# Attention and two expert layers on one core: new homes for S, P V and layer 1 in PSUM, joint transposes, a new order

## The chip, the cores and the metric

The kernel runs on one core of a Trainium2 chip. The metric is device time in microseconds of one execution. A core has TensorE (PE, with its weight load as PEld), VectorE (DVE), ScalarE (ACT), GpSimd (POOL) and SyncE (SP, which here only issues transfers); DVE, ACT and TensorE reach PSUM, which has eight banks of 512 float32 columns in each of 128 partitions.

## The reference, cut to what matters

```python
q_rot, k_rot = rotate(q), rotate(k)            # batch 4, heads 8, seq 576, head_dim 64
scores = matmul(q_rot, k_rot^T) / sqrt(64); scores -= max(scores)
attn = exp(scores); attn /= sum(attn) + 1e-9
x = matmul(attn, v)                            # as 2304 tokens x 512
h = x @ w_in;  g = h * clip(h + 3, 0, 6) / 6;  y = g @ w_out          # 512 -> 2048 -> 512
h = y @ w_in2; P = a0 + a1 h + a2 h^2 + a3 h^3; Q = 1 + |b0||h| + |b1| h^2
out = (P / (Q + 1e-6)) @ w_out2                                       # 512 -> 2048 -> 512
```

All inputs are float32. The kernel keeps the accuracy by splitting values into a high and a low half (16-bit in attention and layer 1, fp32r in layer 2) and multiplying high by high, high by low and low by high.

## The kernel before

**Attention.** The 8 heads of a batch are 4 pairs. `prep_qk` loads a pair's k and q (`nat`), sums their squares for a scale, rotates them on DVE (buffer `ropea`), writes the high and low halves of each into `qk16` and sends each through a DMA transpose (L818); `k2` is k with its halves swapped. `prep_v` splits v. `unit` is one block of 128 queries of both heads of a pair (a fifth unit of each pair takes the 64 last queries of both): S = q k into PSUM (L856), the row maximum on DVE (L862), one small operation on it (L864, on POOL), the exponential on ACT (L869, tile `e`), the high half `p16h` (L539, L541 or L543 by engine), the low half `p16l` on DVE (L881), a DMA transpose of each half (L878) and P V (L898, L901), whose result and row sums ACT or DVE copy to `xu`. There are 5 units for each of 16 pairs, 80 in all. `x_out` divides by the sums, splits x and transposes both halves (L937).

**Layer 1** (`layer1`) follows in two parts for each batch, of 256 and 320 columns: 16 blocks of 12 matmuls (L968), each taken out of PSUM by ACT (L972) and DVE (L974) and split into `gh` and `gl`; then 4 output groups of 48 matmuls (L992). Its weights are loaded as raw 32-bit words and decoded exactly by ACT and DVE (L636 to L639), then split (L646). **Layer 2** runs at the end, 5 blocks of columns by 16 steps, and reuses the memory of both.

**PSUM.** S has one tile of 2560 columns, five banks; unit i uses columns 0 to 1151 or 1280 to 2431 by turns:

```python
sbank = tl("psa", [128, 2560], F32, "s")
obank = tl("psa", [128, 512], F32, "ob")
c0 = 1280 * (i % 2)
```

One more bank, `ob`, holds P V at three places by turns and the results of small sums over partitions (`small`, `total`); layer 1 has two banks `h`.

**The order.** Every operation is given to a planner (`Plan`) with the engines that may run it, a cost for each and a due time in ticks of 4000 ns. `Plan.order` plays the program forward: each free engine takes the ready operation with the earliest due time, and a second engine of the list may take it at a penalty `pen`. The order that comes out is the order of the instructions in each engine's queue; what an instruction waits for on the chip is found from the data. The table `PR` holds the engines (`'GA'` is POOL, then ACT; Q is SP's queue), buffer numbers and shifts of the due times by operation (`o_...`, and `z_...` for the first batch). `EN(key)` takes the entry with a 0 at its end for the first two batches.

Of the kernel before, what the change touches and what calls it, by code (L numbers as in the profile page):

```python
# [22 lines left out]
S = 576  # L23
# [14 lines left out]
PR = {'c01': -1.023,  # L38
# [3 lines left out]
 'e_ev': 'AD',  # L42
 'e_ev0': 'AD',
 'e_gh': 'GD',
# [3 lines left out]
 'e_hi': 'ADG',  # L48
 'e_hi0': 'ADG',
 'e_mx': 'G',  # L50
 'e_mx0': 'G',
 'e_ob': 'A',
 'e_qk': 'GA',
 'e_qk0': 'GA',
# [6 lines left out]
 'e_v': 'DG',  # L61
 'e_v0': 'GAD',
 'e_vl': 'D',
 'e_vl0': 'D',
 'e_w': 'G',
 'e_wl': 'D',
 'e_wl0': 'D',
 'e_xh': 'A',
# [5 lines left out]
 'e_y': 'A',  # L74
 'e_y0': 'A',
# [5 lines left out]
 'l0q': 0.5,  # L81
 'l1o': 2.462,
 'l1p': -2.749,
 'lead': 14.779,
 'lead0': 7.701,
# [4 lines left out]
 'o_': -43.42,  # L90
 'o_ab': -2.87,
 'o_ac0': -118.75,
 'o_ac1': 0.34,
 'o_ac2': -86.97,
 'o_ac3': 94.5,
 'o_acc': 17.25,
 'o_bb': -12.47,
 'o_d': -49.02,
 'o_e': -40.44,
 'o_f32': -13.78,  # L100
 'o_g2l': -17.75,
 'o_gh': 39.63,
 'o_gl': 7.33,
 'o_h': 3.68,
 'o_h2': 12,
 'o_half': 66.6,
 'o_hh': 3.05,
 'o_hr': 11.75,
 'o_hx': 2.17,
 'o_ident': 138.79,  # L110
 'o_k2': 20.81,
 'o_lgh': 53.65,
 'o_lgl': -159.43,
 'o_lq': -53.65,
 'o_lr': -2.25,
 'o_ls': -34.29,
 'o_lt': 4.25,
 'o_mx': 12.06,
 'o_na': -45.2,
 'o_nat': 6.15,  # L120
 'o_ob': -0.02,
 'o_ones': 72.16,
 'o_p1': -5.5,
 'o_p16': 0.25,
 'o_p16h': 32.49,
 'o_p16l': 0.33,
 'o_pt': 6.74,
 'o_pth': -4.52,
 'o_ptl': -9.92,
 'o_pw': 35.47,  # L130
 'o_pwi': -44.5,
 'o_qal': -73.87,
 'o_qam': -26.95,
 'o_qb': -48.22,
 'o_qk16': 4.58,
 'o_qpi': -3.4,
 'o_qps': 10.25,
 'o_qpv': -48.65,
 'o_r': -29.58,
 'o_r0': 18,  # L140
 'o_raw': -4.11,
 'o_ropea': 20.61,
 'o_ropeb': 4.5,
 'o_s': -0.66,
 'o_so': -46.98,
 'o_t': -203.65,
 'o_t0': 28.3,
 'o_t1': 0.14,
 'o_tab': -87.11,
 'o_u': -23,  # L150
 'o_v9': 25.68,
 'o_vam': 118.58,
 'o_vm4': 36.12,
 'o_vnat': 9,
 'o_vnat0': 12.82,
 'o_vnat1': -27.04,
 'o_vpi': -56.08,
 'o_vps': -35.07,
 'o_vpv': -77.42,
 'o_vqi': 6.84,  # L160
 'o_vqs': -58.99,
# [24 lines left out]
 'o_y1d': -133.22,
# [28 lines left out]
 'w20': 109.798,  # L215
 'w21': 121.496,
# [3 lines left out]
 'wi0': -8.964,  # L220
 'wi1': 4.619,
 'wo0': -2.418,
 'wo1': 6.01,
 'y0': 2,
 'z_': 2.02,
 'z_ab': -15.43,
 'z_ac0': -6.16,
 'z_ac1': -16.43,
 'z_ac2': -25.19,
 'z_ac3': -7.09,  # L230
 'z_acc': 0.0,
 'z_bb': 20.23,
 'z_d': 16.19,
 'z_e': 1.8,
 'z_f32': 8.07,
 'z_g2h': 0.0,
 'z_gh': -14.04,
 'z_gl': -0.51,
 'z_h': 0.0,
 'z_h2': 0.0,  # L240
 'z_half': -10.82,
 'z_hh': -8.5,
 'z_hr': 0.0,
 'z_hx': 3.93,
 'z_ident': -8.76,
 'z_k2': 26.21,
 'z_lgh': -1.25,
 'z_lgl': 17.55,
 'z_lq': 6.06,
 'z_lr': -1.93,  # L250
 'z_ls': -16.45,
 'z_lt': -3.17,
 'z_mx': -0.03,
 'z_na': -20.82,
 'z_nat': -0.01,
 'z_ob': 0.06,
 'z_ones': -25.61,
 'z_p1': 0.0,
 'z_p16': 0.0,
 'z_p16h': -11.01,  # L260
 'z_p16l': 0.0,
 'z_pt': 0.0,
 'z_pth': 0.89,
 'z_ptl': -8.13,
 'z_pw': 2.56,
 'z_pwi': -3.9,
 'z_qal': 0.48,
 'z_qam': 3.82,
 'z_qb': -8.89,
 'z_qk16': -5.39,  # L270
 'z_qpi': 6.81,
 'z_qps': -13.66,
 'z_qpv': -1.31,
 'z_r': 5.16,
 'z_r0': 0.0,
 'z_raw': 3.72,
 'z_ropea': 0.0,
 'z_s': 0.0,
 'z_so': 2.72,
 'z_t': -13.02,  # L280
 'z_t0': 2.23,
 'z_t1': -0.22,
 'z_tab': 1.34,
 'z_u': 0.0,
 'z_v9': -0.53,
 'z_vam': 22.59,
 'z_vm4': -1.37,
 'z_vnat': 0.0,
 'z_vnat0': -0.34,
 'z_vnat1': 11.21,  # L290
 'z_vpi': 3.94,
 'z_vps': 2.18,
 'z_vpv': -0.76,
 'z_vqi': 0.09,
 'z_vqs': -3.6,
 'z_vqv': -0.13,
 'z_vv': 0.0,
 'z_w0_': -1.91,
 'z_w1_': -1.69,
 'z_w2_': -11.93,  # L300
 'z_w2d': -53.68,
 'z_w2s': 0.31,
 'z_wam': 0.46,
 'z_wao': -23.4,
 'z_woi': -19.0,
 'z_wos': -20.61,
 'z_wov': -28.27,
 'z_wpi': 19.44,
 'z_wps': 3.61,
 'z_x20': -25.98,  # L310
 'z_x21': -5.61,
 'z_xf': 0.57,
 'z_xh': -0.37,
 'z_xl': -1.14,
 'z_xn': 0.0,
 'z_xt': -3.31,
 'z_xu': 0.87,
 'z_y0': 0.0,
 'z_y1': 0.65,
 'z_y1d': 19.64}  # L320
# [13 lines left out]
class Til:  # L334


    def __init__(self, plan, pool, shape, dtype, tag, bufs):
        self.plan, self.pool, self.shape, self.dtype, self.tag, self.bufs = plan, pool, shape, dtype, tag, bufs
        self.ops, self.last, self.t = [], {}, None
        plan.tags.setdefault((pool, tag), []).append(self)  # L340

    def __call__(self):
        if self.t is None:
            self.t = self.plan.pools[self.pool].tile(self.shape, self.dtype, tag=self.tag, name=self.tag, bufs=self.bufs)
        return self.t


class Op:
    __slots__ = ("engs", "cost", "fn", "prio", "deps", "outs", "then", "left", "dma", "ready", "idx", "end", "lat", "st", "eng", "why", "nm")


class Plan:
# [5 lines left out]
    def __init__(self):  # L358
        self.ops, self.tags, self.pools, self.prio, self.used, self.first, self.early = [], {}, {}, 0.0, {}, True, True

    def tile(self, pool, shape, dtype, tag, bufs=1):
        return Til(self, pool, shape, dtype, tag, bufs)

    def op(self, engs, cost, fn, r=(), w=(), lat=None, prio=None):

        o = Op()
        o.engs, o.fn, o.deps, o.idx = engs, fn, set(), len(self.ops)
# [8 lines left out]
        for writes, keys in ((False, r), (True, w)):  # L376
            for key in keys:
                t, part = key if isinstance(key, tuple) else (key, None)
                if isinstance(t, Til):
                    t.ops.append(o)  # L380
                    self.used.setdefault(t.pool, []).append(o)
# [15 lines left out]
    def order(self):  # L397
        first = []
        for ts in self.tags.values():
            ts = [t for t in ts if t.ops]  # L400
            for n, t in enumerate(ts):
# [3 lines left out]
                if n >= t.bufs:  # L405
                    for x in t.ops:
                        x.deps.update(y for y in ts[n - t.bufs].ops if y is not x)
        for o in self.ops:
            o.outs, o.then, o.left, o.ready = [], [], len(o.deps), 0.0
# [12 lines left out]
        taken = set()  # L422
# [9 lines left out]
        t = hwdge = 0.0  # L432
        win, edge, busy, slow = 3413.0, 3413.0, 0.0, 2.0
        while len(result) < len(self.ops):
            moved = True
            while moved:
                moved = False
                for e in "NPADGQ":
                    while ready[e] and (e == "N" or free[e] <= t):
                        _, _, o = heapq.heappop(ready[e])  # L440
                        if o.idx in taken:
                            continue
                        taken.add(o.idx)
# [9 lines left out]
                        elif o.dma:  # L453
                            hw, hold = o.dma[:2]
                            hwdge = max(hwdge, t + (60 if e == "A" else 0)) + hw
                            dma = max(dma, hwdge + 650)
                            free[e] = dma + 80 if len(o.dma) > 2 else hwdge + (50 if e == "A" else 0)
                            dma += hold
                            end = dma + 950
# [812 lines left out]
```

## Time and profile before

| what | us |
|---|---|
| median of 3 runs | 1159.66 |
| the runs | 1156.73, 1159.66, 1162.18 |
| span of the profiled execution, first to last instruction | 1155.4 |
| TensorE busy | 992.8 (86% of the span) |
| DVE busy | 945.8 (82%) |
| ACT busy | 671.4 (58%) |
| POOL busy | 243.6 (21%) |

The profile is of one execution, and its span is the time that can be split by stage; of its own time nothing else is recorded, and the timed runs stand 1.3 to 6.8 us above it. Shares are means over stages with different limits: attention and layer 1 lie between 0 and about 740 us, layer 2 behind.

### The profile page before, as it was taken

To read this page: it belongs to the slowest core of one execution; us is meant where nothing else is said; L and a number is where in the kernel's file an instruction comes from. 1 tells how busy PE (TensorE), PEld (TensorE's weight loads), DVE (VectorE), ACT (ScalarE), POOL (GpSimd) and SP (SyncE) were. 2 spreads that over 40 slices of the span, in tenths; PEclk is the share of its full clock that TensorE was granted. 3 is DMA by queue.
4 is the path that set the end of the run, shared out by engine and by line. 5 is a ranking of instruction groups with operands and counts; after the bars stand their busy time and mean duration, and the time that the engine had idled before them with its cause. 6 is when DMAs were issued, how large, how long until landed. Compare 5 with 4: busy or idle time off the path is not lost. (4 is left out here: it accounts for less than half of the span.)

```text
span 1155.4 us, 21512 instructions
## 1 busy us (share of the span) xinstructions
PE 992.8 (86%) x8102; PEld 789.0 (68%) x8102; DVE 945.8 (82%) x1707; ACT 671.4 (58%) x1230; POOL 243.6 (21%) x288
## 2 busy tenths in 40 slices
PE   1243577788998898999989999989999999999997
PEld 0132366566677766778667887768888888888885
DVE  5888899898888887798885838589988888888887
ACT  5544674455355475454444624587776776676676
POOL 0534247644333332252321300000000000000000
PEclk9976598899999999999999999999999999999999
DMA  7986997687788986888888874812120020010010
GB/s 219 229 211 140 212 216 144 148 164 158 136 160 156 171 154 142 175 162 193 147 160 180 177 179 145 271 55 65 46 55 10 10 55 1 3 35 10 1 37 19
DMA packets 299047, 142.96 MB, mean 124 GB/s; under 512 B 246720, under 2 KB 280128, under 8 KB 298944
## 3 DMA queue, kind: packets, MB, share of 16 engines
q1 hardware_dynamic: 294304, 135.38, 54.5%
q10 hardware_dynamic: 4640, 6.23, 2.1%
q8 instruction: 63, 1.03, 0.4%
q14 instruction: 40, 0.33, 0.1%
HBM read 61.33 MB, written 17.83 MB: 69 GB/s over the span
## 5 line engine op out<-in xcount | busy, mean ns | idle before, releaser
L968 PE MATMUL h<-xt,w 128*128 128x256 f16 (+1 forms) x1536 | 204.7, 289 | 12.7 <-DVE t L974 12.6
L992 PE MATMUL h<-gh,w 128*128 128x256 f16 (+1 forms) x960 | 191.6, 288 | 1.0 <-DVE w L646 1.0
L968 PEld LDWEIGHTS <-w 128*128 128x128 f16 x1536 | 149.9, 99 | 53.8 <-issue 14.7
L1175 PE MATMUL ac<-w,lgh 128*128 128x512 f32 x576 | 179.5, 392 | 3.1 <-ACT lgh L1165 2.4
L869 ACT ACTIVATE e<-s,mx,qal 128x576 f32<-128x576 f32 (+1 forms) x144 | 115.6, 833 | 110.3 <-DVE mx L862 35.5
L992 PEld LDWEIGHTS <-w 128*128 128x128 f16 x1440 | 139.6, 99 | 37.3 <-DVE w L646 1.3
L992 PE MATMUL h<-gl,w 128*128 128x256 f16 (+1 forms) x480 | 138.2, 288 | 0.0
L862 DVE TENSOR_REDUCE mx<-s 128x2 f32<-128x1152 f32 (+1 forms) x80 | 99.4, 1245 | 41.7 <-PE s L856 22.8
L856 PE MATMUL s<-t,t 128*128 128x192 f16 (+9 forms) x360 | 88.8, 302 | 50.8 <-ACT e L869 28.9
L1175 PEld LDWEIGHTS ac<-w,lgh 128*128 128x128 f32 x576 | 106.8, 188 | 28.3 <-ACT lgh L1165 3.8
L856 PEld LDWEIGHTS <-t 128*128 128x128 f16 (+1 forms) x720 | 62.7, 110 | 86.5 <-issue 58.5
L1142 PE MATMUL hh<-x,w 128*128 128x512 f32 (+1 forms) x516 | 117.6, 377 | 2.8 <-DVE lt L1157 2.8
L1175 PE MATMUL ac<-w,lgl 128*128 128x512 f32 x288 | 113.2, 393 | 0.0
L881 DVE TENSOR_TENSOR p16l<-e,p16h 128x1152 f16<-128x1152 f32 (+1 forms) x80 | 102.2, 1277 | 12.3 <-DMA ptl<-p16l 12.1
L1142 PEld LDWEIGHTS hh<-x,w 128*128 128x128 f32 x516 | 91.8, 190 | 23.8 <-DVE lt L1157 4.5
L972 ACT ACTIVATE t<-h,half,d 128x256 f32<-128x256 f32 (+1 forms) x128 | 74.8, 586 | 52.7 <-PE h L968 49.6
L1142 PE MATMUL hx<-x,w 128*128 128x512 f32 (+1 forms) x444 | 98.0, 370 | 0.0
L864 POOL TENSOR_SCALAR mx<-mx,qal 128x2 f32<-128x2 f32 (+1 forms) x80 | 57.7, 721 | 172.0 <-DVE mx L862 132.6
L1142 PEld LDWEIGHTS hx<-x,w 128*128 128x128 f32 x444 | 77.3, 188 | 16.1
L898 PE MATMUL ob<-v,pth 128*128 128x65 f16 (+1 forms) x800 | 77.3, 200 | 11.8 <-DMA pth<-p16h 10.5
L856 PE MATMUL s<-k,t 128*128 128x192 f16 (+9 forms) x360 | 86.6, 303 | 0.0
L541 POOL TENSOR_SCALAR gh<-t 128x256 f16<-128x256 f32 (+1 forms) x90 | 56.9, 636 | 130.9 <-DVE t L974 124.1
(130 smaller groups left out, 1944.8 us busy)
## 6 DMA issues: line engine op xcount, KB each, us to landing
raw<-in_moe_w_in_dram SPq DMA_DIRECT2D x32, 512.0 KB, 4.6
raw<-in_moe_w_out_dram SPq DMA_DIRECT2D x32, 512.0 KB, 4.2
w2d<-f SPq DMA_DIRECT2D x32, 256.0 KB, 4.2
w2s<-w2d SPq DMA_DIRECT2D x32, 256.0 KB, 2.8
out_dram<-ob SPq DMA_DIRECT2D x36, 128.0 KB, 2.4
vnat<-in_v_dram SPq DMA_DIRECT2D x16, 256.0 KB, 3.1
nat<-in_k_dram SPq DMA_DIRECT2D x32, 128.0 KB, 2.5
nat<-in_q_dram SPq DMA_DIRECT2D x32, 128.0 KB, 2.4
```

The lines of the kernel that those rows point to most:

```text
L541: pool.tensor_scalar(out, in_, scale, 0.0, ALU.mult, ALU.add)
L856: pe.matmul(sbank()[r0:r0 + m, x:y], lhsT=qq[:, q0:q0 + m], rhs=kk[:, kx:kx + y - x], start=(j == 0), stop=(j == 1))
L862: op("D", c_dve(n), lambda e: vec.reduce_max(mx()[:, 0, 0:g], sv().rearrange("p (g n) -> p g n", g=g), axis=AX.X), r=[s], w=[(mx, 0)])
L864: op(EN("e_mx"), {"D": 170, "G": 270}, lambda e: EL[e].tensor_scalar(mx()[:, 1, 0:g], mx()[:, 0, 0:g], al()[:, 1:2], float(LSH * np.log(2. ...
L869: op("A", c_act(n // g, 2, False), lambda e, h=h: act.activation(et()[:, h * (n // g):(h + 1) * (n // g)], sv()[:, h * (n // g):(h + 1) * ...
L881: op(EN("lo"), c_sub(n), lambda e: EL[e].tensor_tensor(lo()[:, 0:n], et()[:, 0:n], ph()[:, 0:n], ALU.subtract), r=es + [ph], w=[lo])
L898: pe.matmul(ob()[0:m, o:o + D + 1], lhsT=w, rhs=vv[:, 0], start=(z == 0 and j == 0), stop=(z == 1 and j == 4))
L968: pe.matmul(hp()[:, 0:N], lhsT=w[:, z, kk], rhs=xt()[:, kk, 0:N], start=(n == 0), stop=(n == 11))
L972: op("A", c_act(N, 2, False), lambda e, t=t, hp=hp, f=f: act.activation(t()[:, 0:N], hp()[:, 0:N], AF.Relu, bias=half(), scale=d()[:, f:f ...
L992: pe.matmul(yp()[:, 0:N], lhsT=w[:, s_, m * 128:(m + 1) * 128], rhs=gt()[:, f, 0:N], start=(f == 0 and z == 0), stop=(f == KF - 1 and z == 2))
L1142: pe.matmul(hp()[:, 0:n], lhsT=w[:, kk], rhs=xt()[:, kk, 0:n], start=(i == 0), stop=(i == 11))
L1175: pe.matmul(accs[j][i]()[0:m], lhsT=gt()[:, x:x + m], rhs=wt(), start=(f == 0 and z == 0), stop=(f == KF - 1 and z == 2))
```

## The change

- S gets two tiles of 1536 columns, three banks each. The two banks left are `h0` and `h1`; each user (a block or output group of layer 1, a P V, a small sum) takes a whole one from the planner when it is free (`Plan.bank`) and gives it back after its last reader.
- P's two halves stand in one tile `p16` of which there are two, and one DMA transpose takes both. The same for x's two halves, and for q and k of a pair (not for the first pair, `apart`). The halves of q and k are written over `ropea` instead of a buffer of their own. k and q come with three transfers each instead of four.
- The planner's costs are new: those of transfers (issue, hold, lead, landing), POOL, waits between engines. `PR` is new throughout, so that the whole order and the choice of engines differ: the small operation on the maximum is on DVE in the first two batches and on DVE or POOL after; `p16h` is on POOL alone in the last two; `gh` there on DVE or ACT instead of POOL or DVE; v on ACT. The loads of y for layer 2 are issued from ACT's queue instead of SP's.

```diff
- 'e_ev': 'AD',  'e_ev0': 'AD',  'e_gh': 'GD',  'e_hi': 'ADG', 'e_mx': 'G',  'e_mx0': 'G',
+ 'e_ev': 'DA',  'e_ev0': 'DA',  'e_gh': 'DA',  'e_hi': 'G',   'e_mx': 'DG', 'e_mx0': 'D',
- 'e_qk': 'GA',  'e_qk0': 'GA',  'e_v': 'DG',   'e_v0': 'GAD', 'e_w': 'G',   'e_xh': 'A',  'e_y': 'A',
+ 'e_qk': 'G',   'e_qk0': 'AG',  'e_v': 'A',    'e_v0': 'AD',  'e_w': 'GD',  'e_xh': 'GA', 'e_y': 'AD',
- 'pen': 7.418, 'pv': 6.419, 'q_k2': 'QA', 'q_y1': 'Q', 'q_y1d': 'AQ',
+ 'pen': 70.376, 'pv': 6.126, 'q_k2': 'AQ', 'q_y1': 'A', 'q_y1d': 'QA', 'apart': 1, 'rp': 1,
- 'lead': 14.779, 'lead0': 7.701, 's0': -13.557, 'step0': 0.971, 'wi0': -8.964, 'wi1': 4.619, 'wo0': -2.418, 'wo1': 6.01,
+ 'lead': 14.042, 'lead0': 96.378, 's0': -34.796, 'step0': 66.414, 'wi0': 115.544, 'wi1': 7.632, 'wo0': -10.426, 'wo1': -28.273,
...
+    def bank(self, tag):
+        t = Til(self, "psh", None, None, tag, 0)
+        self.rows.setdefault(tag, []).append(t)
+        return t
...
+                        if o.need is not None:
+                            if not spare:
+                                late.append(o)
+                                taken.add(o.idx)
+                                continue
+                            o.need.bank = spare.pop(0)
...
+def turn_cost(nb):
+    return (1210 + 13 * nb, 150 * nb, 180, 1870)
...
-    sbank = tl("psa", [128, 2560], F32, "s")
-    obank = tl("psa", [128, 512], F32, "ob")
+    sbank = [tl("psa", [128, 1536], F32, "s", 2) for _ in range(2)]
+    pl.banks = [pl.pools["psh"].tile([128, 512], F32, tag=f"h{i}", name=f"h{i}") for i in range(2)]
...
-    def small(n, kind=0):
-        c = 400 + kind * 32
-        return (obank, c), lambda: obank()[:, c:c + n]
+    def small(n):
+        t = pl.bank("hs")
+        return t, lambda: t()[:, 0:n]
...
-            w = tl("attn", [128, NB, 2 * D], F16, "qk16", PR["qk"])
+        def w():
+            return tb().rearrange("p i j d -> p (i j d)").bitcast(F16).rearrange("p (i j e) -> p i j e", i=2, j=NB)
...
-        ph, lo = (tl("attn", [128, 2 * S], F16, "p16" + z, n_) for z, n_ in (("h", PR["p16"]), ("l", PR["p16l"])))
-        th, tlo = (tl("attn", [128, NB, 128], F16, "pt" + z, PR["pt"]) for z in "hl")
+        ph = tl("attn", [128, 4 * S], F16, "p16", PR["p16"])
+        th = tl("attn", [128, 2 * NB, 128], F16, "pt", PR["pt"])
-        turn(ph, th)
-        turn(lo, tlo)
+        op("Q", turn_cost(2 * nb), lambda e: DE[e].dma_start_transpose(out=th()[:, 0:2 * nb], in_=ph()[:, 0:2 * n]), r=[ph], w=[th])
-        ob = obank
-        o0 = i % 3 * 2 * (D + 1)
+        ob = pl.bank("ob")
...
-            hp = tl("psh", [128, 512], F32, "h", 2)
+            hp = pl.bank("h")
```

## Rows read from the trace of the kernel before

**Rows 1.** Busy us of each engine by stage (windows), granted clock, DMA share, GB/s.
```profile
0.00:29.00 29.00, 2.91 (x10) 2.50 (x10) 14.99 (x59) 14.74 (x32) 2.87 (x7) 1.00 0.76 219
...
core 0: us, PE busy (x) PEld busy (x) DVE busy (x) ACT busy (x) POOL busy (x), PEclk, DMA share, GB/s
0.00:290.00 290.00, 167.62 (x1719) 128.99 (x1720) 245.55 (x464) 151.59 (x306) 120.61 (x125) 0.86 0.82 184
290.00:690.00 400.00, 370.89 (x4188) 295.29 (x4186) 311.24 (x569) 198.74 (x344) 120.61 (x160) 0.99 0.84 163
690.00:1156.00 466.00, 454.30 (x2199) 364.73 (x2196) 388.97 (x675) 321.06 (x580) 2.40 (x3) 0.99 0.19 52
```

**Rows 2.** What TensorE waited for, 0 to 290 us: total, times, longest.
```profile
PE s L856 <- ACT e L869: 22.3, 9, 4.0
PE s L856 <- DVE mx L862: 12.0, 6, 4.8
```

**Rows 3.** The same, 290 to 690 us.
```profile
PE s L856 <- DVE mx L862: 7.2, 5, 2.5
PE h L968 <- DVE t L974: 7.0, 10, 2.2
PE s L856 <- ACT e L869: 6.6, 8, 1.3
```

**Rows 4.** What DVE waited for, 0 to 290 us.
```profile
DVE w L638 <- ACT w L636: 13.8, 7, 5.6
DVE mx L862 <- ACT e L869: 8.7, 6, 3.5
...
DVE p16l L881 <- DMA ptl<-p16l: 1.0, 2, 0.8
```

**Rows 5.** Timeline, 450 to 462 us: start, duration, operation, idle before it.
```profile
451.81 0.19 PE L898 MATMUL ob<-v,pth 128*128 128x65 f16 x1
...
451.91 1.75 POOL L864 TENSOR_SCALAR mx<-mx,qal 128x2 f32<-128x2 f32 x1 [4.02 <-DVE mx L862]
...
453.08 1.27 SPq L878 DMA_TRANSPOSE ptl<-p16l  x1
...
453.52 0.28 DVE L543 COPY xu<-ob 128x130 f32<-128x130 f32 x1
...
453.69 1.55 ACT L869 ACTIVATE e<-s,mx,qal 128x576 f32<-128x576 f32 x2 [3.65 <-POOL mx L864]
...
455.27 1.36 DVE L862 TENSOR_REDUCE mx<-s 128x2 f32<-128x1152 f32 x1 [1.40 <-ACT e L869]
...
456.55 0.14 DVE L609 TENSOR_SCALAR vqv<-vqi 128x1 f32<-128x1 f32 x1
...
456.68 0.27 PE L856 MATMUL s<-t,t 128*64 128x256 f16 x1 [1.92 <-DVE vqv L609]
```

**Rows 6.** Groups of POOL, 29 to 290 us: busy us, mean ns, idle before.
```profile
L864 POOL TENSOR_SCALAR mx<-mx,qal 128x2 f32<-128x2 f32 (+1 forms) x29 | 24.5, 844 | 55.1 <-DVE mx L862 39.5 <-DVE vqv L609 12.7 <-DMA pth<-p16h 2.3
```

**Rows 7.** Groups of DVE, 0 to 290 us; then one line's durations (min/median/max ns), whole run.
```profile
L814 DVE SCALAR_TENSOR_TENSOR qk<-nat,qps,qk 128x576 f16<-128x576 f32 x16 | 15.5, 970 | 2.5 <-POOL qk L541 2.5
...
L609 DVE TENSOR_SCALAR qpv<-qpi 128x2 f32<-128x2 f32 x9 | 2.2, 239 | 0.0
...
L814 DVE SCALAR_TENSOR_TENSOR qk<-nat,qps,qk x32: 778/812/1690, 23.7 to 544.5; 128x576 f16<-128x576 f32 x32
```

**Rows 8.** Chain, groups by form, and the P V tile (290 to 690 us).
```profile
714.81 13.04 PE h L992 x96
...
L972 ACT ACTIVATE t<-h,half,d 128x320 f32<-128x320 f32 x64 | 39.3, 613 | 32.8 <-PE h L968 31.7 <-ACT junk L654 0.3
...
L974 DVE SCALAR_TENSOR_TENSOR t<-t,h 128x320 f32<-128x320 f32 x64 | 30.6, 480 | 8.9 <-ACT t L972 8.6
...
L898 PE MATMUL ob<-v,pth x530: 191/193/262, 297.1 to 681.7; 128*128 128x65 f16 x137, 128*64 128x65 f16 x40
```

**Rows 9.** Transfers by line: count, us from issue to landing.
```profile
pth<-p16h SPq DMA_TRANSPOSE x80, 3.6
```

More of the change, by code (lines that the diff above doesn't have):

```diff
@@ L34 @@
 NM = PARTS[1][1]
[L38 removed]
+PR = {'apart': 1,
+ 'c01': -66.968,
  'e': 2,
@@ new lines @@
+ 'o_hh': -147.34,
+ 'o_hr': -682.66,
+ 'o_hs': 2.41,
+ 'o_hx': 1.86,
+ 'o_ident': 518.24,
+ 'o_k2': 54.37,
+ 'o_lgh': 447.41,
+ 'o_lgl': -957.84,
+ 'o_lq': -305.39,
+ 'o_lr': -449.58,
+ 'o_ls': -305.24,
+ 'o_lt': 4.3,
+ 'o_mx': -4.6,
+ 'o_na': 254.19,
+ 'o_nat': -15.52,
+ 'o_ob': 1.32,
+ 'o_ones': 30.01,
+ 'o_p1': 248.15,
+ 'o_p16': 197.12,
+ 'o_p16h': 103.5,
+ 'o_p16l': -903.0,
+ 'o_pt': -140.85,
+ 'o_pth': 693.62,
+ 'o_ptl': -77.78,
+ 'o_pw': 182.18,
+ 'o_pwi': -279.11,
+ 'o_qal': -260.1,
+ 'o_qam': -388.58,
@@ new lines @@
+ 'z_gl': 199.8,
+ 'z_h': 1.21,
+ 'z_h2': -292.87,
+ 'z_half': 269.25,
+ 'z_hh': -224.67,
+ 'z_hr': -927.6,
+ 'z_hs': -644.52,
+ 'z_hx': 320.41,
+ 'z_ident': 365.39,
+ 'z_k2': 471.38,
+ 'z_lgh': 262.0,
+ 'z_lgl': -668.2,
+ 'z_lq': -599.27,
+ 'z_lr': 216.61,
+ 'z_ls': -655.63,
+ 'z_lt': 377.33,
+ 'z_mx': 108.4,
+ 'z_na': -299.82,
+ 'z_nat': -93.43,
+ 'z_ob': -226.46,
+ 'z_ones': -77.74,
+ 'z_p1': -142.13,
+ 'z_p16': -207.0,
+ 'z_p16h': -251.99,
+ 'z_p16l': 692.03,
+ 'z_pt': -60.68,
+ 'z_pth': 675.77,
@@ L338, in __init__ @@
         self.plan, self.pool, self.shape, self.dtype, self.tag, self.bufs = plan, pool, shape, dtype, tag, bufs
-        self.ops, self.last, self.t = [], {}, None
-        plan.tags.setdefault((pool, tag), []).append(self)
+        self.ops, self.last, self.t, self.bank, self.open = [], {}, None, None, 0
+        if bufs:
+            plan.tags.setdefault((pool, tag), []).append(self)
     def __call__(self):
+        if not self.bufs:
+            return self.plan.banks[self.bank]
         if self.t is None:
@@ L348 @@
 class Op:
-    __slots__ = ("engs", "cost", "fn", "prio", "deps", "outs", "then", "left", "dma", "ready", "idx", "end", "lat", "st", "eng", "why", "nm")
+    __slots__ = ("engs", "cost", "fn", "prio", "deps", "outs", "then", "left", "dma", "ready", "idx", "end", "lat", "st", "eng", "why", "nm", "need", "held", "own")
 class Plan:
@@ L379, in op @@
                 if isinstance(t, Til):
+                    if not t.bufs and o not in t.ops:
+                        if not t.ops:
+                            o.need = t
+                        o.held.append(t)
+                        t.open += 1
                     t.ops.append(o)
@@ L407, in order @@
                         x.deps.update(y for y in ts[n - t.bufs].ops if y is not x)
+        for tag in ("h", "ob"):
+            ts = self.rows[tag]
+            first += [(x.ops[0], y.ops[0]) for x, y in zip(ts, ts[1:])]
         for o in self.ops:
@@ L421, in order @@
         result = []
-        taken = set()
+        taken, spare, late = set(), list(range(len(self.banks))), []
         def push(o):
@@ L453, in order @@
                         elif o.dma:
[L454 to L459, printed above, removed]
+                            issue, hold, lead, after = o.dma
+                            begin = max(dma, t + lead)
+                            free[e] = max(t + issue, begin - lead)
+                            dma = begin + hold
+                            end = dma + after
                         else:
@@ L485, in order @@
                 _, _, o, outs = heapq.heappop(events)
+                if o.held and not (outs and outs is o.own):
+                    for x in o.held:
+                        x.open -= 1
+                        if not x.open:
+                            spare.append(x.bank)
+                            for y in late:
+                                taken.discard(y.idx)
+                                push(y)
+                            late.clear()
                 for x in outs:
```

617 lines of the change are left out of this document (290 added, 327 removed).

## The prediction

> **What bounds the kernel now.** I read the three stages first [rows 1]. From 690 us to the end TensorE is busy 454.3 of 466 us at a granted clock of 0.99: that is layer 2 and the rest of layer 1, bound by TensorE, and no part of the change takes matmuls away. From 290 to 690 it is busy 370.9 of 400 us. From 0 to 290 it is busy only 167.6 us, at a mean clock of 0.86 of 2.4 GHz, while DVE is busy 245.6 us. So the loss lies in the start (290 - 167.6 = 122 us idle), about 29 us more lie in the middle, and 12 us in the rest. A start in which DVE is busy 15.0 us of the first 29, and 230.6 of the next 261 (88%), is bound by DVE: the work that feeds TensorE (weights decoded and split, q/k turned, row maxima, low halves of P) passes through it. What a change can win in the start is DVE's idle time, 30.4 us after the first 29 us and 14 us within them; what it can win in the middle is TensorE's 29 us.
>
> Next I read the waits. TensorE's own S matmuls wait for the exponential (22.3 us) and for the row maximum (12.0 us) in the start [rows 2], and for the same two 6.6 and 7.2 us in the middle, where layer 1 waits another 7.0 us for DVE [rows 3]. DVE in the start waits 13.8 us for ACT's decode, 8.7 us for the exponential of another unit before it takes a maximum, and 1.0 us for the transpose that still reads the only buffer of P's low half [rows 4].
>
> The wait of a maximum for an exponential is no dependence of the computation. A piece of the timeline shows where it comes from [rows 5]: ACT's two exponentials of one unit run from 453.69 to 455.24; DVE's maximum over the next unit's S, which has long been written, begins at 455.27, after 1.40 us idle; it ends at 456.63, and TensorE's next S matmul begins at 456.68, after 1.92 us idle. The two S buffers are 1280 columns each in one tile, so they meet in the third of its five banks of 512 columns. The three engines take turns in that bank, and a double buffer works partly as a single one. The Trainium skill, page "PSUM — Partial Sum Buffer", section "PSUM bank collisions raise a hardware error", says that no two of TensorE, ScalarE and VectorE may touch one bank (of the same partitions) at once, reads against reads included, and that software has to keep them apart by bank. These rows agree: 0.03 and 0.05 us lie between the end of one engine's access and the start of the next one's.
>
> **The change, part by part, start of the kernel.** S in two buffers of three whole banks ends the turns between units. On DVE that gives back the 8.7 us [rows 4]; TensorE's 12.0 us are the same time seen from the other side and are not added, since DVE sets the pace here. P's halves in one buffer of two copies take away the 1.0 us. Of DVE's other idle time in the start, 30.4 - 9.7 = 20.7 us (13.8 of it behind the decode), the new order can win anything from nothing to all of it, and a worse order could lose as much; the diff moves weights, q/k preparation and their engines, so I take half, 10.3 us. Together 20 us.
>
> Against it stands the small operation on the maximum, once per unit, 80 times in all; 29 of them fall in the start, on POOL at 844 ns [rows 6], and in the first two batches it is now on DVE. DVE's nearest row, a two-column tensor_scalar in the same stretch, has 239 ns, and one in the middle 140 ns [rows 5, 7]: 29 units times 0.24 is 7.0 us at most, times 0.14 it is 4.1. I take 5.5. In return POOL, which shares work with DVE in this stretch, loses the 24.5 us of this one operation. The q/k split on DVE is 970 ns in the start against a median of 812 over the run [rows 7]: 16 times 0.16 is 2.5 us, and the like for other operations beside POOL. I take 3 us (0 to 8). The first 29 us, 14 us of DVE idle, I leave alone (0 to 7): first loads have to land whatever the order. Start: 20 - 5.5 + 3 = 17.5 us.
>
> **Middle.** S no longer waits for another unit's maximum: 7.2 us. Of its 6.6 us behind the exponential I take half, 3.3, since the wait for its own buffer's reader stays. Of the 7.0 us behind DVE's layer-1 step, half, 3.5, as DVE loses turns too. That is 14 us of 29. The maximum's small operation, the other 51 times at 0.14 to 0.24 us, is 7 to 12 us of DVE, hidden by DVE's 89 us of idle time here; without that cover it would cost just this. The wait for POOL that it removes lies in the chain from S to P, and the pieces at 451.91 (1.75 us on POOL for two columns) show how long it can be; the chain has the lead that the plan gives P V, so I count nothing.
>
> Now the other side of the PSUM edit. Before, layer 1 had two banks of its own and P V with the small sums a third; after, all share two. A block of layer 1 for 320 columns holds a bank for its matmuls (13.04 us for 96 is 1.63 for twelve), ACT's 0.61 and DVE's 0.48 and two handovers, about 3.1 us; for 256 columns some four fifths, 2.6. The four output groups are four such blocks of matmuls and one evacuation, about 7.3 and 6.0 us [rows 8]. A batch has 16 + 16 of the first and 4 + 4 of the second: 91 + 53 = 144 us of bank time. P V held its bank from 451.81 to 453.80, 2.0 us [rows 5], 20 times: 40 us. The middle does 53 P V (530 matmuls with the high half and V's high part, ten each) in 400 us, so a batch takes 151 us [rows 8], and two banks give 302. The load rises from 144 to 184 of 302, from 48% to 61%, and every evacuation can still meet a DVE instruction of up to 1.36 us ahead of it. Cost per P V: nothing if S or the other bank's matmuls fill the gap, at most what its bank stays occupied after its matmuls, 2.0 - 1.0 = 1.0 us, so 0 to 53 us. It is nearer to nothing, because the load leaves 118 us free, the order is planned with these two banks, and S matmuls need neither: 0.1 us each, 5 us. Middle: 14 - 5 = 9 us.
>
> **DMA.** The transposes fall from 160 + 64 + 32 = 256 to 80 + 32 + 17 = 129. One costs SP 1.27 us to issue [rows 5], so SP gains some 160 us; nothing in rows 2 to 4 ends with SP, so I count it as nothing (a loss is excluded by the count alone, unless the longer one blocks the queue, 0.2 to 1.3 us each behind it). The joint one starts only when the low half is done and moves twice the blocks: P lands 3.6 us after issue now [rows 9], later between 3.6 and 7.2. P V is planned about six ticks of 4 us behind, 24 us, which hides it. Writing q/k's halves over the rotation's own buffer makes the next pair's rotation wait for that transpose; pairs are some 16 us apart after the first, and DVE has the decode to do meanwhile, so nothing (at most three times 5 us in the first batch). The loads of y now stand in ACT's queue, ahead of layer 2's activations: 20 issues at 1.27 us at most is 25 us, ACT is idle for 145 us in that stage [rows 1]: nothing, unless one waits long at the head.
>
> **The sum.** 17.5 + 9 = 26.5 us from the span of 1155.4 gives 1128.9. The three timed runs (median 1159.66) lie 1.3 to 6.8 us above that span, the median 4.3, and 1128.9 + 4.3 is 1133. The last stage (12 us of TensorE idle) is taken as it is. Predicted: 1133 us, 2.3% less than the median.
>
> **Rivals.** First, a better one: the new order closes nearly all of DVE's idle time in the start (30 - 5.5 + 8 + 7 of the first 29) and 25 of TensorE's 29 us in the middle: 39 + 25 = 64 us, 1096 us. For it speaks that both waits come from a bank the old order took for two; against it, that DVE also waits for ACT's decode, which stays. Second, on the other side: the two shared banks become the bound. With 1.0 us per P V the middle loses 53 us against 14 won; with the start's 17.5 the net is +21.5, 1181 us. It decides from 31.5 / 53 = 0.6 us per P V on; at 0.75 it is 8 us slower, 1168. For it speak the DVE queue (an instruction of 1.36 us ahead of an evacuation) and a small sum of a few columns that now takes a whole bank; against it the 118 us of free bank time per batch. The skill's bank rule stands behind this one too: what shares a bank takes turns, however few columns it has. Third, no change: DVE's start keeps its length because the operations moved onto it (5.5 to 7 us) and a longer decode wait eat the 9.7 us, and the middle's gain is lost to the banks: 1155 to 1164.
>
> **How the numbers follow.** Forecast 0.52 (its own range 1112 to 1150, by the halves taken as a quarter or three quarters and the banks at 0 to 0.3 us), the better order 0.20, the banks 0.18, no change 0.10. A measurement of this kernel tells 0.5%, 5.8 us, from no change. Faster: 0.52 + 0.20 and a little of the third case's lower edge, 0.73; same 0.10; slower 0.17. The range takes in most of both neighbours: 1092 to 1168.
>
> **What would show it.** Right: no wait of a maximum for another unit's exponential, and TensorE's wait for the maximum near 0; DVE's idle time between 29 and 290 us below 15 us; TensorE above 380 of 400 us in the middle; 129 transposes. Wrong: TensorE's layer 1 or P V waiting for evacuations of the shared banks by more than 20 us; ACT waiting for loads of y; DVE's busy time in the start above 255 us; a start in which TensorE's steady work begins later than about 230 us.

## The result: 1168.5 us, 0.9% slower

Four runs of the changed kernel gave 1166.58 to 1170.87 us, median 1168.49, against a median of 1158.89 for the kernel before on the same chip: ratio 1.0092, 95% interval [1.0066, 1.0119]. The forecast was 1133 us with a range of 1092 to 1168, and faster with a chance of 0.73. Its direction was wrong. The time is the number of the second rival (the shared banks at 0.75 us for each P V: 1168), though not by its sum: the start gave less than the 17.5 us that stand in it.

The stages of the changed kernel (windows, columns as in [rows 1]):

```profile
core 0: us, PE busy (x) PEld busy (x) DVE busy (x) ACT busy (x) POOL busy (x), PEclk, DMA share, GB/s
0.00:29.00 29.00, 2.78 (x10) 2.43 (x10) 20.53 (x69) 15.69 (x35) 3.45 (x7) 1.00 0.93 254
0.00:290.00 290.00, 175.67 (x1797) 129.50 (x1798) 263.21 (x526) 165.43 (x317) 82.91 (x80) 0.85 0.87 197
290.00:690.00 400.00, 357.64 (x3928) 275.72 (x3926) 306.68 (x584) 191.90 (x356) 109.88 (x120) 0.98 0.81 165
690.00:1167.00 477.00, 466.33 (x2370) 379.42 (x2366) 385.12 (x652) 326.57 (x592) 0.00 (x0) 0.99 0.16 42
```

Beside [rows 1]: in the start TensorE is busy 8.1 us more and does 1797 matmuls instead of 1719; in the middle it is busy 13.3 us less and does 3928 instead of 4188. So 182 matmuls fewer are done by 690 us, and the stage behind has 12.0 us more of TensorE's work. The start did gain; the middle lost more.

TensorE's waits, 0 to 290 us, then 290 to 690 us (answers to [rows 2, 3]):

```profile
...
PE h L956 <- DMA pt<-p: 14.5, 8, 4.8
...
PE s L919 <- ACT e L932: 9.8, 8, 2.8
...
PE h L1025 <- DVE t L1031: 5.6, 9, 1.8
...
PE h L956 <- DVE t L1031: 2.4, 1, 2.4
```

```profile
PE h L956 <- DMA pt<-p: 13.4, 9, 3.0
PE h L1025 <- DVE t L1031: 11.5, 13, 3.1
PE h L956 <- DVE t L1031: 2.8, 5, 1.1
PE h L956 <- ACT t L591: 1.7, 1, 1.7
...
PE s L919 <- ACT e L932: 0.8, 2, 0.4
```

S's waits went as the diff says: for the maximum 12.0 and 7.2 us became none in the list, for the exponential 22.3 and 6.6 became 9.8 and 0.8. In their place stand waits of the two shared banks `h`: layer 1 for DVE's evacuation 11.5 us in the middle (7.0 before), P V for layer 1's evacuation (L956 behind L1031, L591), which it never met in its own bank, and P V for P's transpose, 13.4 us in the middle. The kernel before waited 2.9 us for that there:

```profile
PE ob L898 <- DMA ptl<-p16l: 2.9, 2, 2.1
```

Over the first 690 us the waits for layer 1's evacuation grew from 12.6 us (`L968`) to 24.1 (17.2 at `L1025`, 5.2 and 1.7 at `L956`), and those of P V for transposes from 15.2 (10.5 and 4.7 for the two halves) to 27.8.

How a shared bank makes P V wait is seen in one piece (timeline, 600 to 605 us):

```profile
600.23 3.15 PE L1025 MATMUL h<-xt,w 128*128 128x320 f16 x22
...
602.29 0.62 ACT L1029 ACTIVATE t<-h,half,d 128x320 f32<-128x320 f32 x1
602.74 0.21 DVE L979 TENSOR_SCALAR r<-xu,xf 128x4 f32<-128x4 f32 x1
...
603.19 0.48 DVE L1034 TENSOR_TENSOR gl<-t,gh 128x320 f16<-128x320 f32 x1
...
603.59 0.41 DVE L982 TENSOR_TENSOR xu<-xu,r 128x256 f32<-128x256 f32 x1
603.93 0.47 DVE L1031 SCALAR_TENSOR_TENSOR t<-t,h 128x320 f32<-128x320 f32 x1
...
604.45 0.19 PE L956 MATMUL h<-v,pt 128*128 128x65 f16 x1 [1.07 <-DVE t L1031]
```

Layer 1's matmuls end at 603.38. ACT is done with the first of the two blocks at 602.91, but DVE takes seven other operations from 602.74 on (three of them shown) and frees the bank only at 604.40. P V begins 0.05 us later, after 1.07 us of idle TensorE. The next matmuls, those of an S at 605.39, stood behind P V in TensorE's queue. The Trainium skill, page "PSUM — Partial Sum Buffer", section "Engine vs sequencer instructions", says that matmuls start and complete in program order; this piece agrees, with nothing from behind P V begun in the 1.07 us.

DVE's wait for another unit's exponential (8.7 us) is gone from the list; of the wait for the decode 8.2 us is left of 13.8 [rows 4]. The maximum's small operation moved to DVE. DVE's waits, 0 to 290 us, and then its groups there:

```profile
DVE w L689 <- ACT w L687: 8.2, 5, 5.9
```

```profile
L927 DVE TENSOR_SCALAR mx<-mx,qal 128x2 f32<-128x2 f32 (+1 forms) x32 | 8.6, 272 | 0.0
```

P's transposes: the tile's line with min/median/max ns of SP over the whole run, first for one half in the kernel before, then for both in the changed one; last the transfers by line of the changed one, median us to landing ([rows 9] have 3.6):

```profile
L878 SPq DMA_TRANSPOSE pth<-p16h x80: 1199/1311/3290, 48.8 to 670.6; - x80
```

```profile
L942 SPq DMA_TRANSPOSE pt<-p x80: 1324/2838/5426, 54.4 to 688.8; - x80
```

```profile
pt<-p SPq DMA_TRANSPOSE x80, 5.2
```

### The profile page after: what moved, and what is told of

The parts are those of the page before. It is cut to its first block, busy times and chain, and to the rows that moved or that the text cites. A ratio compares the mean times of both kernels' runs of the same rounds, so it can differ in the third digit from the quotient of the medians.

```text
span 1167.0 us, 21142 instructions
## 1 busy us (share of the span) xinstructions
PE 999.6 (86%) x8086; PEld 784.6 (67%) x8086; DVE 955.0 (82%) x1761; ACT 683.9 (59%) x1264; POOL 192.8 (17%) x200
## 5 line engine op out<-in xcount | busy, mean ns | idle before, releaser
L1025 PE MATMUL h<-xt,w 128*128 128x256 f16 (+1 forms) x1536 | 204.6, 289 | 19.9 <-DVE t L1031 17.2
L1025 PEld LDWEIGHTS <-w 128*128 128x128 f16 x1536 | 150.0, 99 | 61.9 <-issue 23.7
L956 PE MATMUL h<-v,pt 128*128 128x65 f16 (+1 forms) x1600 | 98.6, 202 | 50.3 <-DMA pt<-p 28.3
L956 PEld LDWEIGHTS <-pt 128*128 128x128 f16 (+1 forms) x1600 | 91.6, 106 | 51.3 <-DMA pt<-p 48.5
L940 DVE TENSOR_TENSOR p<-e,p 128x1152 f16<-128x1152 f32 (+1 forms) x80 | 102.8, 1288 | 11.3 <-POOL p L593 9.5
L1031 DVE SCALAR_TENSOR_TENSOR t<-t,h 128x256 f32<-128x256 f32 (+1 forms) x128 | 56.9, 446 | 52.9 <-ACT t L1029 51.4
L919 PE MATMUL s<-qkt 128*128 128x512 f16 (+3 forms) x352 | 90.8, 307 | 10.7 <-ACT e L932 10.6
L919 PEld LDWEIGHTS <-qkt 128*128 128x128 f16 (+1 forms) x704 | 57.4, 112 | 59.3 <-issue 29.2
L593 POOL TENSOR_SCALAR p<-e 128x1152 f16<-128x1152 f32 (+1 forms) x55 | 68.4, 1244 | 166.9 <-DMA pt<-p 60.2
```

The lines of the kernel that those rows point to most:

```text
L593: pool.tensor_scalar(out, in_, scale, 0.0, ALU.mult, ALU.add)
L919: pe.matmul(s()[r0:r0 + m, x:y], lhsT=qq[:, q0:q0 + m], rhs=kk[:, kx:kx + y - x], start=(j == 0), stop=(j == 1))
L940: op(EN("lo"), c_sub(n), lambda e: EL[e].tensor_tensor(ph()[:, n:2 * n], et()[:, 0:n], ph()[:, 0:n], ALU.subtract), r=es + [(ph, 0)], w=[( ...
L956: pe.matmul(ob()[0:m, o:o + D + 1], lhsT=w, rhs=vv[:, 0], start=(z == 0 and j == 0), stop=(z == 1 and j == 4))
L1025: pe.matmul(hp()[:, 0:N], lhsT=w[:, z, kk], rhs=xt()[:, kk, y, 0:N], start=(n == 0), stop=(n == 11))
L1031: op("D", c_dve(N), lambda e, t=t, hp=hp: vec.scalar_tensor_tensor(t()[:, 0:N], t()[:, 0:N], two(-15), hp()[:, 0:N], ALU.min, ALU.mult), r ...
```

## The experiments

The suspects: the banks shared, the joint transpose, the new order. "Old order" means that each instruction keeps the engine that it has in the kernel before, and is due at its place there:

```diff
+    for o, x in zip(pl.ops, FOLLOW.split()):   # place and engine of each operation before
+        o.prio, o.engs = float(x[:-1]), x[-1]
```

That fixes the order only where the plan finds an instruction's buffer and data ready at its place; what finds no free bank is put off. By the traces c2 (below) has the old order throughout, but in c3 and b2, which share one order, 949 of DVE's 1707 instructions stand at another place, and in the other runs of the old order some are moved too. The pairs whose instructions stand in one order on every compute engine, so that they differ in their edits alone, are the kernel before and c2, d3 and d2, b1 and c1, c3 and b2, and, in the change's order, the changed kernel with a1 to a5 and c4.

Times are medians, ratios are to the kernel before on the same chip. The edits stand in short form.

**First, from the changed kernel backward.** P's transpose cut in two, the high half's issued as soon as it is written (a1), or both in the place of the joint one (a2); S in the five banks of before, which meet in the third (a3); the same with a third bank for P V and the sums (a4); a3's S, a third bank and two transposes, the new order alone (a5).

```diff
-dma_start_transpose(out=th()[:, 0:2 * nb], in_=ph()[:, 0:2 * n])
+for z in range(2): dma_start_transpose(out=th()[:, z * nb:z * nb + nb], in_=ph()[:, z * n:z * n + n])  # a1, a2, a5
-            return s()[:, 0:n]
+            return five()[:, 1280 * (i % 2):1280 * (i % 2) + n]                                           # a3, a4, a5
+    pl.banks.append(pl.pools["psa"].tile([128, 512], F32, tag="h2", name="h2"))                          # a4, a5
```

> The changed kernel with its order kept, but each unit's P goes through two transposes again: the high half's is issued as soon as the high half is written, the low half's where the joint one stood. Theory D (the joint transpose is the loss: it holds SP's queue 2.8 us in the median and P lands late): TensorE's wait of P V for P, 28 us in all, falls by half or more and the time falls by 8 to 14 us, to about 1157. Theory T (the two PSUM banks that layer 1, P V and the small sums share are the loss): within 4 us of the changed kernel, 1164 to 1172. Theory O (the new order is the loss, whatever the parts): the same, 1164 to 1172.

> The changed kernel with its order kept, each unit's joint transpose cut into two of one half each, both issued where the joint one stood. This has the two short instructions but not the early start of the high half. If what costs is that one long transfer holds the queue and lands as a whole, it gains like the run with the early high half, to about 1157 to 1160. If what costs is the late start, it stays at 1164 to 1172. Theories T and O: 1164 to 1172.

> The changed kernel with its order kept, S back in one tile of five banks whose two buffers meet in the third; the two other banks shared as in the change, one bank left empty. It takes back only the gain of S in banks of its own. Theory T: that gain is real, 10 to 20 us (TensorE waited 19 us for the maximum in the kernel before), so the time rises to 1178 to 1190. Theory O or D: the order hides it, less than 5 us, 1165 to 1174.

> As the run with S in five banks, and the bank left empty given to P V and the small sums; layer 1 has the two others, where the order allows it. The difference to the run with S in five banks is the price of two shared banks against three. Theory T: 12 to 25 us faster than that run, TensorE's waits for evacuations ahead of P V and of layer 1 fall from about 25 us to below 12. Theories D and O: less than 5 us faster.

> The new order and engines without the structure: S in five shared banks, a third bank for P V and small sums, each unit's P in two transposes with the high half early. Theory O: the losses add up, about 1196 plus 9, 1198 to 1210, some 45 us slower than before, which is then the price of the new order. Theory T, second form: 1175 to 1195, since a good part of the order's loss should be given back by the third bank.

| run | us | ratio, interval |
|---|---|---|
| a1 | 1177.52 | 1.0177 [1.0138, 1.0217] |
| a2 | 1175.16 | 1.0149 [1.0107, 1.0191] |
| a3 | 1192.65 | 1.0304 [1.0271, 1.0337] |
| a4 | 1196.00 | 1.0327 [1.0289, 1.0366] |
| a5 | 1201.15 | 1.0362 [1.0324, 1.0399] |

Each undoing made it slower. So neither the joint transpose (worth 7 to 9 us here; a2's interval touches the changed kernel's) nor S in its own banks (24 us) is what loses. a5 came within what had been expected if the new order is the loss (1198 to 1210); but it runs an order planned for two banks and joint transposes without them, so it is no fair price of that order. A third bank gave nothing back (a3 to a4). P V's waits until 690 us, in a3, then in a4, where the second line is gone:

```profile
PE h L959 <- DMA pt<-p: 31.5, 15, 7.5
PE h L959 <- DVE t L1034: 7.2, 7, 2.5
```

```profile
PE h L959 <- DMA pt<-p: 37.2, 19, 7.1
```

So with the order kept, the waits behind the shared banks went and others took their place. This does not clear the sharing, since the order had been planned with two banks. What was missing was the other direction.

**Then, from the kernel before forward, in the old order.** The joint transpose (b1; it brings two copies of P's halves, and q/k's halves over `ropea`); the PSUM plan of the change (b2); both (b3); the two shared banks with S left in five (c3).

```diff
-        turn(ph, th)
-        turn(lo, tlo)
+        dma_start_transpose(out=t2_()[:, 0:2 * nb], in_=p2()[:, 0:2 * n])        # b1, b3
-        ob = obank
+        ob = pl.bank("ob")                                                       # b2, b3, c3
-            hp = tl("psh", [128, 512], F32, "h", 2)
+            hp = pl.bank("h")                                                    # b2, b3, c3
-    sbank = tl("psa", [128, 2560], F32, "s")
+    sbank = [tl("psa", [128, 1536], F32, "s", 2) for _ in range(2)]              # b2, b3
```

> The kernel before with its order and engines kept (each operation due at its old place), and the joint transpose of P's halves alone, with the two-copy tile for them; q/k's halves stand over the rotation's buffer to make room. The runs under the new order gave the joint transpose a gain of 7 to 9 us. If the parts help and the new order loses (theory O): faster than before by 3 to 12 us, 1147 to 1156. If the joint transpose only helps where the order was planned for it: 1158 to 1172.

> The kernel before with its order and engines kept as far as the banks allow, and the new PSUM plan alone: S in three banks each, layer 1, P V and small sums sharing two. Theory O: the gain of 24 us that S in its own banks showed under the new order is seen here too, at least in part: 1135 to 1153. Theory T in a second form (the scarcity of banks costs in the order that it forces, not in waits on the chip): slower than before, 1165 to 1195.

> Both of the above, old order: the new PSUM plan and the joint transpose of P. This is nearly the whole change without the new order and engine choices. Theory O: 1125 to 1150, well below the changed kernel's 1168. Theory T, second form: 1165 to 1195.

> Old order; layer 1, P V and small sums share two banks, S stays in its five, one bank stays empty. The other half of the PSUM edit by itself. Theory T: slower than the run with the whole PSUM edit (1184.6) by what S in its own banks gives back there, 1190 to 1205. If S's own banks give nothing under the old order: 1180 to 1188.

| run | us | ratio, interval |
|---|---|---|
| b1, joint transpose | 1154.43 | 0.9965 [0.9945, 0.9986] |
| b2, PSUM plan | 1184.57 | 1.0228 [1.0198, 1.0257] |
| b3, both | 1166.46 | 1.0071 [1.0044, 1.0097] |
| c3, sharing alone | 1203.81 | 1.0403 [1.0356, 1.0450] |

This points at the sharing: b1 came within the range for gainful parts (1147 to 1156), b2 and b3 within those for too few banks (1165 to 1195), c3 within its own (1190 to 1205). With S as it was, it costs 1203.8 - 1157.9 = 46 us, and in that the order which the plan makes for two banks is included: no run tells the waits at the banks from that order. S in its own banks gives 19 us back (c3 to b2, one order), the joint transpose with its buffers and its order 18 more (b2 to b3), and what is then left is the changed kernel's time within 2 us, without its table `PR`. Of c3's 46 us, 31 are idle time of TensorE before 690 us; 10 are longer busy time for the same work (1002.8 us instead of 992.8), at a granted clock of 0.79 instead of 0.86 in the first 290 us. The stages of c3, and its waits from 290 to 690 us:

```profile
0.00:290.00 290.00, 154.40 (x1526) 117.61 (x1526) 233.78 (x441) 141.88 (x290) 117.98 (x114) 0.79 0.80 175
290.00:690.00 400.00, 353.21 (x3915) 275.49 (x3916) 302.18 (x551) 195.35 (x337) 132.25 (x162) 0.98 0.80 159
```

```profile
PE h L1266 <- DVE t L1272: 13.6, 17, 2.4
PE s L1154 <- ACT e L1167: 12.9, 11, 2.3
PE h L1196 <- DVE t L1272: 8.1, 5, 3.1
```

TensorE's busy time is 13.2 us behind [rows 1] by 290 us and loses 17.7 more by 690. Layer 1 and P V wait 21.7 us for DVE's evacuation of layer 1 in the middle, against 7.0 in [rows 3]. S's wait for the exponential grew too, from 6.6 to 12.9 us, though S's own banks are those of before.

**S in its own banks without sharing.** S needs 1152 of its 1536 columns, so P V and the small sums fit into the empty ones; layer 1 keeps two banks for itself. In the old order alone (c2), with the joint transpose (c1); in the change's order (c4).

```diff
+    s3 = [tl("psa", [128, 1536], F32, f"s3{x}") for x in range(2)]
-        o0 = i % 3 * 2 * (D + 1)
+        o0 = 1152 + i % 3 // 2 * 2 * (D + 1)
+        at_s = s3[i % 3 % 2]          # P V's place: behind S, in either tile
```

> The same without the joint transpose: S in three banks each, P V and small sums in S's empty columns, layer 1 in its own two banks, old order. Theory T: 1143 to 1154, TensorE's waits of S for the maximum and the exponential (48 us in all before) fall by half. Otherwise 1155 to 1168.

> Old order and engines, S in three banks each, but P V and the small sums stand in the columns that S leaves empty in its third banks, so that layer 1 keeps its two banks; with the joint transpose of P. Theory T (the loss is that layer 1 shares its banks; S in its own banks and the joint transpose are gains): 1138 to 1150, faster than before and than the joint transpose alone (1154). If turns in S's third banks with P V and the sums cost as much as the old third bank did: 1152 to 1162.

> The changed kernel with its order kept, joint transposes and S in three banks each as in the change, but P V and the small sums stand in S's empty columns, so that layer 1 alone has the two banks. Theory T: the waits of TensorE for evacuations of the shared banks (some 20 us in the middle) fall by half and the time to 1150 to 1162. Theory O, or if turns in S's third banks cost as much: 1164 to 1176.

| run | us | ratio, interval |
|---|---|---|
| c2 | 1144.48 | 0.9896 [0.9851, 0.9942] |
| c1 | 1150.53 | 0.9939 [0.9919, 0.9959] |
| c4 | 1179.40 | 1.0200 [1.0167, 1.0234] |

c2 has the lowest time of this study, below both kernels; its order is the old one throughout, so this is the placement alone. Its stages, and its waits from 290 to 690 us:

```profile
0.00:290.00 290.00, 174.42 (x1739) 128.31 (x1740) 248.69 (x474) 152.76 (x308) 121.11 (x126) 0.82 0.86 186
290.00:690.00 400.00, 379.94 (x4233) 295.99 (x4232) 314.49 (x580) 202.22 (x351) 121.97 (x161) 1.00 0.85 166
```

```profile
PE h L1231 <- DVE t L1237: 7.9, 14, 1.3
PE s L1118 <- ACT e L1131: 2.0, 3, 0.9
PE s L1161 <- DVE mx L1124: 1.6, 2, 1.1
PE s L1118 <- ACT xu L800: 1.6, 2, 1.3
...
PE s L1161 <- ACT e L1131: 1.4, 3, 0.8
```

TensorE is busy 379.9 of 400 us in the middle, 9.0 us more than in [rows 1], which is the sum that the prediction gave the middle. S's 13.8 us of waits in [rows 3] are down to 2.0 behind the exponential; for standing in S's banks P V (L1161) pays 1.6 us behind a maximum and 1.4 behind an exponential, and S 1.6 behind P V's copy to `xu`. The Trainium skill, page "PSUM — Partial Sum Buffer", section "PSUM bank collisions raise a hardware error", states the rule that the prediction cites for any columns of a bank. By it P V's place here must cost turns with S, and the run agrees that it does: 4.6 us in the middle. So S's share of the reasoning holds, once nothing takes it away again.

c4 missed what was forecast for it (1150 to 1162 if the sharing was the loss): in the change's order the same placement is about 11 us slower than the two shared banks. P V then waits 30.2 us for S's readers until 690 us, against 13.1 in c2:

```profile
PE s L961 <- ACT e L937: 21.1, 10, 8.2
...
PE s L961 <- DVE mx L930: 9.1, 7, 2.1
```

```profile
PE s L1161 <- DVE mx L1124: 8.3, 6, 3.2
...
PE s L1161 <- ACT e L1131: 4.8, 5, 2.6
```

So in the change's order the empty columns cost more than they save, and c4 cannot say what the sharing costs in the changed kernel.

**The two copies without the joint transpose.** In the old order: the low half's two copies and q/k over `ropea` alone (d3), and on top of c2 (d2).

```diff
- 'p16l': 1,
+ 'p16l': 2,
-            w = tl("attn", [128, NB, 2 * D], F16, "qk16", PR["qk"])
+            w = tb()[:, i] ... .bitcast(F16)        # over the rotation's buffer
```

> The kernel before with P's low half in two copies and the q/k halves written over the rotation's buffer, nothing else; two transposes. The one joint transpose, with the same two copies, took 1154.4 us against 1159.3. If the second copy was what gained: 1152 to 1157. If the joint transpose was: 1158 to 1162.

> Old order; S in three banks each, P V and the small sums in S's empty columns, layer 1 in its own two banks (the run that took 1144.5 us), and now P's low half in two copies and the q/k halves written over the rotation's buffer; two transposes as before. If the joint transpose's gain under the old order (5 us) was the second copy: 1137 to 1142. If it was the transpose: 1142 to 1147, no different from 1144.5.

d3 took 1162.75 us, 1.0060 [1.0035, 1.0086]; d2 1147.33 us, 0.9937 [0.9916, 0.9958]. With the order that comes of them, the buffers gain nothing: 0.6% slower in before's banks (d3), and behind c2 about 0.4%, where the intervals overlap. The joint transpose, again with its order, then gains about 0.9% in before's banks (0.9965 against 1.0060, d3 to b1) and nothing in S's empty columns (d2 to c1, 0.9937 and 0.9939). Whether that gain is the transpose's or the order's is not shown.

**The new order.** It had been planned under two shared banks. Planned anew for S in its own banks, P V in the empty columns and the joint transpose (d4). Then with the planner's cost of a joint transpose of 18 blocks (of 128 by 128 values), 1.44 us of SP, raised to 2.74 us, near the 2.84 us of the trace (the median of all joint ones; those of 18 blocks have 3.15): without sharing (e2), and for the changed kernel's own banks (e1).

```diff
-    return (1210 + 13 * nb, 150 * nb, 180, 1870)
+    return (1210 + 170 * max(0, nb - 9), 150 * nb, 180, 1870 + 90 * max(0, nb - 9))   # e1, e2
```

> The new planner and the joint transpose, S in three banks each, P V and the small sums in S's empty columns, layer 1 in its own two banks, and the order and the engine choices planned anew for this placement (the planner's numbers set anew too). If the new order gains nothing only because it was planned under two shared banks: 1135 to 1152, at or below the same placement in the old order with the joint transpose (1150.5). If the new way of planning loses time whatever the banks, or the turns that P V now takes with S cost more than its plan sees: 1160 to 1185 (the new order with this placement, not planned anew, took 1179.4).

> The changed kernel with its buffers, banks and transposes, but planned anew with the joint transpose at the issue time that the trace shows: the planner's cost of a transpose of 18 blocks goes from 1.44 to 2.74 us on SP and its landing 0.8 us later; the planner's numbers were set anew for it. If the new order gains nothing because P V was planned too close behind transposes that the plan takes for shorter than they are: TensorE waits under 14 us for them before 690 us (28 us in the changed kernel) and the time falls to 1145 to 1160. If that is a side effect and the order costs its gain by something else: 1163 to 1195, whatever those waits do.

> The same cost of the joint transpose, with S in three banks each, P V and the small sums in S's empty columns and layer 1 in its own two banks, planned anew. The run before it with this placement, planned with the shorter cost, took 1192.8 us and waited 36 us for transposes before 690 us. If the plan's cost of the transpose was what lost it: waits under 15 us and 1145 to 1165. If the order loses by other things: 1170 to 1195.

| run | us | ratio, interval |
|---|---|---|
| d4 | 1192.82 | 1.0320 [1.0285, 1.0354] |
| e2 | 1175.10 | 1.0139 [1.0082, 1.0196] |
| e1 | 1173.05 | 1.0117 [1.0050, 1.0184] |

TensorE's waits before 690 us: for the joint transpose in d4; P V's (`L966`) and layer 1's in e2; P V's for the joint transpose in the changed kernel and in e1:

```profile
PE s L966 <- DMA pt<-p: 35.7, 21, 11.0
```

```profile
PE s L966 <- DVE mx L935: 19.0, 9, 4.2
PE s L966 <- ACT e L942: 13.9, 11, 3.6
PE s L966 <- DMA pt<-p: 13.9, 9, 3.0
PE h L1035 <- DVE t L1041: 12.2, 18, 1.8
```

```profile
PE h L956 <- DMA pt<-p: 27.8, 17, 4.8
```

```profile
PE h L956 <- DMA pt<-p: 17.8, 11, 6.2
```

Planning without the sharing did not make the new order gain: d4 is 42 us slower than the same banks and transposes in the old order (c1). With the transpose's cost near the measured one, the wait falls from 35.7 to 13.9 us and the time by 18 us. That speaks for that cost as a part of d4's loss, but does not show it, since e2's table `PR` differs from d4's elsewhere too. e2 is still 25 us behind c1, though its wait fell below the 15 us that had been forecast with 1145 to 1165. P V waits 32.9 us for S's readers in it. The plan does not count these turns, since it takes P V's columns and S's for separate places. In the change's own banks the same repair cut the wait from 27.8 to 17.8 us and gained nothing. Each of these tables came from a search of limited length, so they show that the plans tried lose, not that every plan would. Why the new way of planning gains nothing stays open beyond these turns.

## Why the prediction was wrong, point by point

**The step that failed** is "0.1 us each, 5 us" for P V in the two shared banks. The bounds were 0 to 1.0 us for each; the value taken was the one near nothing, because 118 us of bank time for a batch were free. In c3, where sharing is the only part of the change, it costs 46 us, more than the 31.5 at which the forecast itself said that the sign turns. Three things were wrong in it. Free time on average is no free bank at the moment: the piece at 604 us shows a bank held 1.5 us beyond ACT's part, by DVE's queue. S matmuls did not fill that gap: they stood behind P V in TensorE's queue. And the price was charged to the middle's 53 P V alone, while c3 has lost 13.2 us of TensorE's busy time by 290 us. That "the order is planned with these two banks" stood in the forecast as a reason for a low price; in c3 that order is a part of the 46 us, and how large a part stays open. Two of the forecast's own signs of being wrong came: the evacuations' waits of 24.1 us, above 20, and DVE's busy time in the start.

**S in its own banks** was right as a mechanism. In the start, TensorE's waits for the maximum and DVE's for the exponential left the lists; in the middle 14 us had been forecast before the banks' price, and c2 shows 9.0 us net with P V in S's banks. Over the whole kernel it is worth 13 us (c2), 19 beside the sharing (c3 to b2) and 24 in the change's order (a3); with the joint transpose, in its order, it is 4 us (b1 to c1), which is not clear of the noise.

**The start**, forecast at 17.5 us, gained 8.1 us of TensorE's busy time. DVE's idle time between 29 and 290 us fell from 30.4 to 18.3 us (261 - (263.21 - 20.53)), not under the 15 that was to show the forecast right; DVE's busy time passed the 255 us that was to show it wrong. The term mis-sized here is the 10.3 us of idle time that "the new order can win": 12.1 us were won in all, where the forecast's three terms add up to 20. The small operation cost 272 ns, not 140 to 240, and 8.6 us for 32 units instead of 5.5 for 29.

**The middle**, forecast at 9 us, lost 13.3. Besides the banks, P V waits 13.4 us for the joint transpose there, 10.5 more than for the halves before, which the sum had at nothing ("24 us, which hides it"). That too was wrong for the changed kernel; in the old order (b3) the same transposes cost P V 11.4 us before 690 us, against 10.5 and 4.7 in the kernel before.

**SP.** The count fell as forecast, but hardly the time: by the sums of the traces the 129 transposes take 340 us of SP, the 256 before took 375; P's 80 joint ones take 234 of them, the 160 single ones took 243. So 35 us were saved and not 160. The sum rightly counted nothing for it; the plan, which counts 1.44 us for 18 blocks, did not.

**The new order** was counted at half of DVE's idle time, 10.3 us. Comparing the changed kernel with b3, whose order comes from the old places, it is worth nothing (1168.5 and 1166.5): it does 111 more matmuls by 290 us and 163 fewer in the middle.

```profile
0.00:290.00 290.00, 167.58 (x1686) 122.83 (x1687) 251.12 (x471) 154.31 (x309) 120.57 (x128) 0.83 0.83 186
290.00:690.00 400.00, 366.86 (x4091) 284.00 (x4088) 310.42 (x559) 194.66 (x340) 114.47 (x157) 0.99 0.79 164
```

These are b3's stages. The first rival (1096) did not come near. The second, the banks as the bound, had the right cause at a chance of 0.18; that its 1168 is the time measured is luck, since its start is 17.5 us and its price is for waits at the banks alone. The third (no change) was nearer than the forecast, and for part of its stated reason: the banks ate the middle's gain.

## What to carry to other kernels

Price a shared buffer by the time from its writer's end until its slowest reader's queue comes round to it, in every stage, and not by its mean load; and count the order that fewer buffers force on a plan. Before giving a producer a bank of its own at the cost of sharing two others, look for columns that are already empty: S's unused columns took P V, and in the old order that kernel was the fastest, while in the change's order the same place lost. Test each part in the old order too: undoing parts of the new one hid the one that cost 46 us. And compare the order of the instructions in the traces, since a run meant to keep it need not.

## What the hardware showed beyond that

- A DMA transpose's time on the issuing queue jumps between 10 and 18 blocks here. Matched in order with the writes of P's low half, the medians are 1.22 us for 5 blocks (16 issues) and 1.31 for 9 (64) in the kernel before, 1.36 for 10 (16) and 3.15 for 18 (64) in the changed one; the median over all 80 hides this. By these medians joining paid on SP for the small fifth units alone. The landing goes from 3.6 [rows 9] to 5.2 us.
- A two-column `tensor_scalar` on the maximum takes 272 ns on DVE and 844 ns on POOL [rows 6], each the mean in its kernel's start.
